# Attention with projections for two problems: weight reloads split by head group, V loads moved to SP's queue, a new order of the first loads

## The chip, the core and the metric

The kernel runs on one core of a Trainium2 chip. Its time is the device time of one execution in microseconds; the median of several executions is compared. TensorE, VectorE, ScalarE and GpSimd (PE, DVE, ACT and POOL in the profile) compute; SyncE (SP) only issues transfers. SP, ACT and POOL each issue DMAs in the order of their own instruction stream, and a wait in such a stream holds everything behind it.

## The reference

Two independent problems A and B of the same shape. Each has 8 batches of 160 queries of width 448, a projection to 16 heads of width 256, cached K and V of 512 positions for each batch and head, and a projection back to 448. All tensors are bfloat16. The results stand side by side in the output (8, 160, 896).

```
q = (x @ wq) -> (B, H, Sq, Dh)
scores = einsum("bhqd,bhkd->bhqk", q, k_cache) * Dh ** -0.5
o = einsum("bhqk,bhkd->bhqd", softmax(scores), v_cache)
out = o -> (B, Sq, H*Dh) @ wo
```

## The kernel before

**Units.** The work is cut into 64 units. A unit is one batch and one head group (4 heads). Two batches form a group (8 units: 4 head groups x 2 batches); problem A has groups 0 to 3, problem B groups 4 to 7. A unit needs one K block (1 MB, loaded by two transposing DMAs, one for each half of the head width, L263) and one V block (1 MB, one copy, L283). K has 6 buffers (`NK`) and is issued 5 units ahead (`DK`); V has 3 buffers (`NV`) and is issued 2 units ahead (`DV`).

**Steps.** The program is written out by hand as one list of tasks for each engine, a loop over steps U = 0 to 63. In step U TensorE computes the scores of unit U (L426, two halves of each head), and between them the product of probabilities and V of unit U-1 (L475 for 128 queries, L500 for the other 32), its row sums (L479, L506), the transposes of the normalised result of unit U-2 (L524, L548), up to 8 chunks of the query projection for the coming group (L320, one chunk is 128 columns of wq), and at the end of the step the output projection of a unit pair three steps back (L358). ScalarE takes the exponential (L439), VectorE empties the accumulators.

**Weights.** One buffer holds wq (`wq_sb`) and one wo (`wo_sb`), for the problem that is being computed. wq of A is loaded by ACT as the first thing (L160, L162). wo of A is issued by SP at step 0, behind the first six K blocks. Problem B's weights replace them: all of wq in 16 DMAs at step 25 (`RELOAD_STEP + 1`, issued by SP when all 128 chunks of problem A are projected), with the chunks of group 4 held back to step 29; all of wo in two halves when every output projection of A is done. One semaphore counts all of wq of a problem and one all of wo, so a consumer waits for the whole matrix.

**Queues.** SP issues K, wq of B and wo. POOL issues x, V and the output. V of unit U waits, on POOL, for its buffer (`pv_done`) and for K of the same unit (`k_sems`):

```
            if U in k_req:
                ksl_, kval_ = k_req[U]
                waits.append((k_sems[ksl_], kval_))
```

**The start.** ACT issues wq, POOL issues x of group 0 and then sets up the identity and ones tiles. SP first waits until wq has landed and then issues K of units 0 to 5 and wo; V of units 0 and 1 follows on POOL. TensorE transposes x of group 0 (L228 and L230, large and small pieces in turn), VectorE copies it (L240, L241), and 8 chunks of the query projection come before the first scores.

Of the kernel before, what the change touches and what calls it, by code (L numbers as in the profile page):

```python
# [33 lines left out]
def bass_concat_heads__mha_block_cached__gqa_block_cached__near_ridge_kernel(  # L34
# [20 lines left out]
    with ExitStack() as es:  # L55
# [42 lines left out]
        oacc_done = S("oacc_done")  # L98
        k_sems = [S(f"k_sem{i}") for i in range(NK)]
        x_sems = [S("x_sem0")]  # L100
        xtr_done = S("xtr_done")
        xevac_done = S("xevac_done")
        wq_sems = [S("wq_sem0"), S("wq_sem1")]
        v_sems = [S(f"v_sem{i}") for i in range(NV)]
        wo_sem = S("wo_sem")
        out_sems = [S("out_sem0")]
        id_sem = S("id_sem")

# [37 lines left out]
                               base=0, pattern=[[-1, 128]], channel_multiplier=1).then_inc(id_sem, 1)  # L146
            pool.memset(wq_sb[0:64, 3, :], 0.0).then_inc(id_sem, 1)

        wq_need = {0: 16 * 4 * 1, 1: 16 * 4 * 4}

        def load_wq(prob_i, cs=(0, 1, 2, 3), split=1):
            prob = probs[prob_i]
            WQB = HD // split

            def body(eng):
                for c in cs:
                    for kb in range(split):
                        cols = slice(kb * WQB, (kb + 1) * WQB)
                        if c < 3:
                            eng.dma_start(wq_sb[:, c, cols], prob["wq"][c * 128:(c + 1) * 128, cols]).then_inc(wq_sems[prob_i], 16)  # L160
                        else:
                            eng.dma_start(wq_sb[64:128, c, cols], prob["wq"][D - 64:D, cols]).then_inc(wq_sems[prob_i], 16)  # L162
            return body

        def load_wo(prob_i, qs=(0, 1, 2, 3)):
            prob = probs[prob_i]

            def body(pool):
                for q in qs:
                    pool.dma_start(  # L170
                        wo_sb[:, q * 8:(q + 1) * 8, :],
                        prob["wo"][q * 1024:(q + 1) * 1024, :].rearrange("(hd p) n -> p hd n", p=128),
                    ).then_inc(wo_sem, 16)
            return body

        x_uses = [0]
# [2 lines left out]
        def issue_x_dma(g):  # L179
            if g >= NGROUPS or ("dma", g) in xg_emitted:  # L180
                return
            xg_emitted[("dma", g)] = True
            prob = probs[g // NG_PER_PROB]
            gb = g % NG_PER_PROB
            xb2 = 0
            waits = []
            if g - 1 >= 0:
                waits.append((xtr_done, g - 1 + 1))
            x_uses[xb2] += 1
            need = 16 * 2 * BG * x_uses[xb2]  # L190

            def body(pool):
                for bl in range(BG):
                    b = gb * BG + bl
                    pool.dma_start(xn_sb[:, xb2, bl, 0, :], prob["x"][b, 0:128, :]).then_inc(x_sems[xb2], 16)
                    pool.dma_start(xn_sb[0:SQ - 128, xb2, bl, 1, :], prob["x"][b, 128:SQ, :]).then_inc(x_sems[xb2], 16)
            task("pool", waits, body)
            return need

        x_need = {}  # L200
# [1 line left out]
        def issue_x(g):  # L202
            if g >= NGROUPS or ("tr", g) in xg_emitted:
                return
            xg_emitted[("tr", g)] = True
            xb2 = 0
            xb = g % NX
            slots = []
            waits = [(x_sems[xb2], x_need[g]), (id_sem, 2)]
            for k2 in range(2):  # L210
                w_, slot = pj_waits()
                waits += w_
                pj_hist.append(("x", g))
                cnt["pj"] += 1
                slots.append(slot)
            if g - NX >= 0:
                waits.append((qproj_done, 32 * (g - NX + 1)))
            pA = pj_banks[slots[0]].bitcast(dt.bfloat16)
            pB = pj_banks[slots[1]].bitcast(dt.bfloat16)

            def pe_body(pe):
                last = None
                for c in range(4):
                    c0 = c * 128 if c < 3 else D - 128
                    dst = pA if c < 3 else pB
                    cb = (c if c < 3 else 0) * NCOL
                    for bl in range(BG):
                        last = pe.transpose(dst[:, cb + bl * SQ:cb + bl * SQ + 128],  # L228
                                            xn_sb[:, xb2, bl, 0, c0:c0 + 128], ident[:, :])
                        last = pe.transpose(dst[:, cb + bl * SQ + 128:cb + (bl + 1) * SQ],  # L230
                                            xn_sb[0:SQ - 128, xb2, bl, 1, c0:c0 + 128], ident[0:SQ - 128, 0:SQ - 128])
                last.then_inc(xtr_done, 1)
            task("pe", waits, pe_body)

            dwaits = [(xtr_done, g + 1)]
            if g - NX >= 0:
                dwaits.append((qproj_done, 32 * (g - NX + 1)))

            def dve_body(dve):
                dve.tensor_copy(xT_sb[:, xb, 0:3, :], pA[:, 0:3 * NCOL].rearrange("p (c n) -> p c n", c=3))  # L240
                dve.tensor_copy(xT_sb[:, xb, 3, :], pB[:, 0:NCOL]).then_inc(xevac_done, 1)  # L241
            task("dve", dwaits, dve_body)
# [21 lines left out]
            task("sp", waits, body)  # L264

        def issue_v(U):
            if U >= NUNITS:
                return
            g, u, hg, bl, prob, b = unit_info(U)
            sl = U % NV  # L270
            waits = []
            if U - NV >= 0:
                waits.append((pv_done, 5 * (U - NV + 1)))
            if U in k_req:
                ksl_, kval_ = k_req[U]
                waits.append((k_sems[ksl_], kval_))
            v_uses[sl] += 1
            v_req[U] = (sl, 16 * v_uses[sl])

            def body(pool):  # L280
                dst = v_sb[:, sl, :, :]
                src = prob["v"][b, hg * HG:(hg + 1) * HG, :, :].rearrange("h (p j) d -> p h (j d)", j=4)
                pool.dma_start(dst, src).then_inc(v_sems[sl], 16)  # L283
            task("pool", waits, body)

        wo_gen = {}

        def pj_waits():
            i = cnt["pj"]
# [13 lines left out]
        def q_chunk(gq, hd):  # L303
            xb = gq % NX
            waits, slot = pj_waits()
            waits.append((xevac_done, gq + 1))
            waits.append((wq_sems[gq // NG_PER_PROB], wq_need[gq // NG_PER_PROB]))
            waits.append((id_sem, 3))
            qi = cnt["qchunk"]
            assert qi // 32 == gq, (qi, gq)  # L310
# [25 lines left out]
        def out_proj(g, hg):  # L336
# [4 lines left out]
            for t in tiles:  # L341
                waits, slot = pj_waits()
                waits.append((otevac_done, 2 * last_unit + 2))
                waits.append((wo_sem, wo_gen[g]))
                oi = cnt["otile"]
                otile_idx[(g, hg, t)] = oi
                pj_hist.append(("o", oi))
# [214 lines left out]
                dve.tensor_copy(o_t, i_t).then_inc(otevac_done, 1)  # L562
            task("dve", dwaits, dve_body)

        for g in range(NGROUPS):
            wo_gen[g] = 64 * (1 + g // NG_PER_PROB)

        task("act", [], load_wq(0))
        x_need[0] = issue_x_dma(0)
        task("pool", [], pool_init)  # L570
        x_need[1] = issue_x_dma(1)
        task("sp", [(wq_sems[0], wq_need[0])], lambda sp: None)
        for U in range(max(DK, DV)):
            if U < DK:
                issue_k(U)
            if U < DV:
                issue_v(U)
        task("act", [(id_sem, 1)], lambda act: act.activation(warm_sb[:, :], ones_sb[:, :], ACTF.Exp, scale=SCALE))
        issue_x(0)
        for hd in range(8):  # L580
# [5 lines left out]
        for gq in range(1, NGROUPS):  # L586
            for hd in range(NHD):
                hgq = hd // 8
                min_step = unit_index(gq - 1, hgq, BG - 1) + 1
                q_queue.append([gq, hd, min_step])  # L590
        RELOAD_STEP = unit_index(NG_PER_PROB - 1, 0, 0)
        for e_ in q_queue:
            if e_[0] == NG_PER_PROB:
                e_[2] = max(e_[2], RELOAD_STEP + 5)
        wq_reloaded = False
        wo_reloaded = False
        oproj_pending = [(g, hg) for g in range(NGROUPS) for hg in range(NHG)]
# [1 line left out]
        for U in range(NUNITS):  # L599
            g, u, hg, bl, prob, b = unit_info(U)  # L600
            cnt["step"] = U
            issue_k(U + DK)
            if U == RELOAD_STEP + 1:
                assert all(not (e_[0] < NG_PER_PROB) for e_ in q_queue), "problem-0 chunks still pending"
                task("sp", [(qevac_done, 32 * NG_PER_PROB)], load_wq(1, (0, 1, 2, 3), split=4))
                wq_reloaded = True
            if U == 0:
                task("sp", [], load_wo(0))
            issue_v(U + DV)
            if u == 2 and g + 2 < NGROUPS:  # L610
                x_need[g + 2] = issue_x_dma(g + 2)
            step_chunks = []
# [23 lines left out]
            for i_ in range(per_block[HG]):  # L636
                q_chunk(*step_chunks.pop(0))
            assert not step_chunks
            while oproj_pending:
                pg, phg = oproj_pending[0]  # L640
                extra = 3 if (pg == NG_PER_PROB and phg == 0) else 0
                if unit_index(pg, phg, BG - 1) + 3 + extra <= U:
                    out_proj(pg, phg)
                    oproj_pending.pop(0)
                else:
                    break
            if wo_reloaded is False and all(((NG_PER_PROB - 1, hh_, 2) in otile_idx) for hh_ in range(NHG)):
                task("sp", [(oacc_done, cnt["oacc"])], load_wo(1, (0, 1)))
                wo_reloaded = U
            elif (wo_reloaded is not False and wo_reloaded is not True):  # L650
                task("sp", [], load_wo(1, (2, 3)))
                wo_reloaded = True

        assert not q_queue
        U = NUNITS
# [6 lines left out]
        otr_tail_task(U - 1)  # L662
        for (pg, phg) in list(oproj_pending):
            out_proj(pg, phg)
        assert wo_reloaded and wq_reloaded

        def final_wait(sp):
            sp.wait_ge(out_sems[0], 16 * out_dma_count[0])
# [43 lines left out]
```

## Time and profile before

| | us |
|---|---|
| median of 6 runs | 707.13 |
| lowest and highest run | 701.29, 726.39 |
| the profiled execution | 695.91 |
| its span | 694.1 |
| TensorE busy in the span | 656.3 (95%) |
| VectorE busy | 443.3 (64%) |
| ScalarE busy | 220.2 (32%) |
| bytes moved by DMA, mean rate | 154.77 MB, 223 GB/s |

The profiled execution is one execution; its own time is 1.8 us longer than the span, which runs from its first to its last recorded instruction. A busy TensorE is not one at its peak: matmuls are pipelined, and its clock can be halved for some microseconds (the PEclk column, 1.00 is the full clock). q1 is the DMA queue of SP, q10 that of ACT, q0 that of POOL. A row "SPq L263" is the time that SP spends on issuing one transposing DMA[...].

### The profile page before, as it was taken

What the parts mean: (1) busy time and instruction counts of PE and PEld (TensorE: products, weight loads), DVE (VectorE), ACT (ScalarE), POOL (GpSimd) and SP (SyncE); (2) the same over time, 40 slices, a digit from 0 to 9 for tenths busy, and PEclk for the clock granted to TensorE, in tenths of its full rate; (3) what the DMA queues carried; (4) which work ended last, traced back from release to release, by engine and by line L of the source; (5) the groups of instructions that cost most, each with busy time, mean ns of one, the idle gap of its engine ahead of it and who ended that gap; (6) DMA issues with size and microseconds to landing.
All of it is one profiled execution on the core that took longest, in us unless ns stands there. A gap on an engine that the chain in (4) does not pass through costs nothing.

```text
span 694.1 us, 19606 instructions
## 1 busy us (share of the span) xinstructions
PE 656.3 (95%) x8576; PEld 521.2 (75%) x8576; DVE 443.3 (64%) x1120; ACT 220.2 (32%) x514; POOL 86.4 (12%) x136
## 2 busy tenths in 40 slices
PE   3799599999999999998999999999999999999985
PEld 1578478787787788786877788778777887788862
DVE  1457457676676667665666677667676667676662
ACT  0223233332333333252322344233323333334420
POOL 4002000020000300020000220002000020001001
PEclk9979989999999999999999999999999999999999
DMA  8999999999999999999999999999999999999500
GB/s 259 224 190 238 299 236 219 242 262 220 246 221 268 242 230 235 213 321 180 185 245 236 233 264 292 247 227 215 262 242 244 199 240 150 222 245 225 173 7 21
DMA packets 297174, 154.77 MB, mean 223 GB/s; under 512 B 268736, under 2 KB 277440, under 8 KB 296640
## 3 DMA queue, kind: packets, MB, share of 16 engines
q1 hardware_dynamic: 276608, 78.14, 70.7%
q0 software_dynamic: 19968, 71.70, 32.8%
q10 hardware_dynamic: 512, 3.67, 1.5%
q8 instruction: 68, 1.11, 0.7%
q14 instruction: 18, 0.15, 0.1%
HBM read 84.08 MB, written 2.29 MB: 124 GB/s over the span
## 4 chain that ended last, share of the span: by engine, by line
PE 85%; SPq 8%; DMA 4%; DVE 1%; issue 1%; POOL 0%; ACTq 0%; POOLq 0%
PE ps L426 20%; PE ps L358 18%; PE ps L320 17%; PE ps L475 15%; SPq L263 8%; PE ps L500 5%; PE ps L524 4%; PE ps L479 3%; DMA wo_sb<-in_A_wo_dram 2%; DMA wq_sb<-in_A_wq_dram 2%; PE ps L548 1%; PE ps L228 1%; PE ps L230 1%; SPq L170 1%; PE ps L506 1%
## 5 line engine op out<-in xcount | busy, mean ns | idle before, releaser
L439 ACT ACTIVATE pT_sb<-ps 128x320 bf16<-128x320 f32 x512 | 218.7, 437 | 447.2 <-PE ps L426 446.4
L426 PE MATMUL ps<-qT_sb,kT_sb 128*128 128x160 bf16 x2048 | 221.4, 235 | 5.1 <-DMA kT_sb<-in_A_k_cache_dram 2.8
L320 PE MATMUL ps<-xT_sb,wq_sb 128*128 128x320 bf16 x1024 | 170.0, 306 | 3.7 <-DVE xT_sb L241 2.7
L426 PEld LDWEIGHTS ps<-qT_sb,kT_sb 128*128 128x128 bf16 x2048 | 154.5, 114 | 14.1 <-DMA kT_sb<-in_A_k_cache_dram 3.5
L457 DVE TENSOR_SCALAR ob_sb<-ps,rc_sb 128x256 bf16<-128x256 f32 x320 | 154.9, 484 | 11.2
L475 PE MATMUL ps<-v_sb,pT_sb 128*128 128x256 bf16 x1024 | 154.6, 274 | 1.3 <-DMA v_sb<-in_A_v_cache_dram 1.3
L330 DVE CAST qT_sb<-ps 128x320 bf16<-128x320 f32 x256 | 125.6, 490 | 38.7 <-PE ps L320 33.9
L320 PEld LDWEIGHTS ps<-xT_sb,wq_sb 128*128 128x128 bf16 x1024 | 95.7, 100 | 35.0 <-DVE xT_sb L241 2.9
L358 PE MATMUL ps<-wo_sb,oT_sb 128*128 128x448 bf16 x512 | 103.9, 357 | 7.9 <-DMA wo_sb<-in_A_wo_dram 7.9
L455 DVE RECIPROCAL rc_sb<-ps 128x1 f32<-128x1 f32 x320 | 53.9, 168 | 80.7 <-PE ps L479 58.3
L475 PEld LDWEIGHTS ps<-v_sb,pT_sb 128*128 128x128 bf16 x1024 | 93.1, 98 | 7.5 <-DMA v_sb<-in_A_v_cache_dram 1.4
L358 PEld LDWEIGHTS ps<-wo_sb,oT_sb 128*128 128x128 bf16 x512 | 50.0, 99 | 52.8 <-issue 10.7
L479 PEld LDWEIGHTS ps<-ones_sb,pT_sb 128*128 128x128 bf16 x1024 | 63.5, 97 | 6.1
L479 PE MATMUL ps<-ones_sb,pT_sb 128*128 128x4 bf16 x1024 | 62.3, 165 | 0.0
L283 POOL DMA_DIRECT2D v_sb<-in_A_v_cache_dram x32 | 24.2, 756 | 282.3 <-PE ps L506 149.7
L283 POOL DMA_DIRECT2D v_sb<-in_B_v_cache_dram x32 | 24.2, 755 | 266.1 <-PE ps L506 226.8
L374 DVE TENSOR_TENSOR oacc_sb<-ps,oacc_sb 128x448 f32<-128x448 f32 x40 | 25.0, 625 | 37.4 <-PE ps L358 37.4
L534 DVE COPY oT_sb<-ps 128x1024 bf16<-128x1024 bf16 x64 | 44.2, 691 | 2.6 <-PE ps L524 0.8
L500 PE MATMUL ps<-v_sb,pT_sb 128*32 128x256 bf16 x1024 | 39.7, 275 | 0.0
L524 PE MATMUL ps<-ident,ob_sb 128*128 128x128 bf16 x512 | 39.1, 219 | 0.5 <-DVE oTt_sb L562 0.5
L524 PEld LDWEIGHTS ps<-ident,ob_sb 128*128 128x128 bf16 x512 | 32.6, 98 | 3.0 <-issue 0.6
L372 DVE COPY oacc_sb<-ps 128x448 f32<-128x448 f32 x20 | 12.5, 625 | 28.3 <-PE ps L358 28.3
(31 smaller groups left out, 241.1 us busy)
## 6 DMA issues: line engine op xcount, KB each, us to landing
v_sb<-in_A_v_cache_dram POOLq DMA_DIRECT2D x32, 1024.0 KB, 8.1
v_sb<-in_B_v_cache_dram POOLq DMA_DIRECT2D x32, 1024.0 KB, 8.1
wo_sb<-in_A_wo_dram SPq DMA_DIRECT2D x4, 896.0 KB, 11.9
wo_sb<-in_B_wo_dram SPq DMA_DIRECT2D x4, 896.0 KB, 8.9
wq_sb<-in_A_wq_dram ACTq DMA_DIRECT2D x3, 1024.0 KB, 7.7
wq_sb<-in_B_wq_dram SPq DMA_DIRECT2D x12, 256.0 KB, 4.9
out_dram<-out_sb POOLq DMA_DIRECT2D x16, 112.0 KB
kT_sb<-in_A_k_cache_dram SPq DMA_TRANSPOSE x64, 8.8
```

What stands on the lines that cost most here:

```text
L263: sp.dma_start_transpose(kT_sb[:, sl, dh, :], src).then_inc(k_sems[sl], 16)
L320: last = pe.matmul(pjb[:, 0:NCOL], wq_sb[:, c, hd * 128:(hd + 1) * 128], xT_sb[:, xb, c, :], start=(c == 0), stop=(c == 3))
L330: dve.tensor_copy(qT_sb[:, hd, :], pjb[:, 0:NCOL]).then_inc(qevac_done, 1)
L358: last = pe.matmul(pjb[0:M, 0:D], stat, wo_sb[:, hd, :], start=(i8 == 0), stop=(i8 == 7))
L426: last = pe.matmul(scb[:, jj * SQ:(jj + 1) * SQ], kt, qT_sb[:, 2 * head + dh, bl * SQ:(bl + 1) * SQ], start=(dh == 0), stop=(dh == 1))
L439: act.activation(pT_sb[:, psl, 2 * half:2 * half + 2, :], scb[:, 0:2 * SQ].rearrange("p (a s) -> p a s", a=2), ACTF.Exp, scale=SCALE).then ...
L455: dve.reciprocal(rc_sb[:, rci:rci + 1], obk[:, DH:DH + 1]).then_inc(rc_sem, 1)
L457: dve.tensor_scalar(out=ob_sb[:, obuf, tile, :], in0=obk[:, 0:DH], scalar1=rc_sb[:, rci:rci + 1], scalar2=None, op0=ALU.mult).then_inc(nor ...
L475: pe.matmul(obk[:, 0:DH], pT_sb[:, psl, jv, 0:128], v_sb[:, vsl, h, jv * DH:(jv + 1) * DH], start=(jv == 0), stop=(jv == 3))
L479: last = pe.matmul(obk[:, DH:DH + NSUM], pT_sb[:, psl, jv, 0:128], ones_sb[:, 0:NSUM], start=(jv == 0), stop=(jv == 3))
L500: pe.matmul(obk[32 * h:32 * (h + 1), 0:DH], pT_sb[:, psl, jv, 128:SQ], v_sb[:, vsl, h, jv * DH:(jv + 1) * DH], start=(jv == 0), stop=(jv = ...
L524: last = pe.transpose(otr_bank[:, (2 * k + dh) * 128:(2 * k + dh + 1) * 128], ob_sb[:, obuf, k, dh * 128:(dh + 1) * 128], ident[:, :])
```

## The change

1. **V moves from POOL to SP** (`issue_v`), and its wait for K of the same unit is dropped. V of unit U now stands in SP's stream directly behind K of unit U+3.
2. **The start is reordered.** x of group 0 is issued by SP as its first DMAs, with a semaphore of its own; K of unit 0 follows without a wait for wq; then SP waits for wq, and V0, K1, V1, V2, K2, wo, K3 and K4 follow. Step 0 adds K5 and step 1 adds K6 and V3.
3. **The reload of wq** is split by head group (`wqB_sem0` to `3`): the four DMAs of head group kb are issued one step after the last chunks of group 3 that read those columns. The projections of group 4 are no longer held back to step 29.
4. **The reload of wo** is split by head group in the same way (`woB_sem0` to `3`), each one step after group 3's output projection of that head group. The output projection of group 4's first head group is no longer held back by three steps.
5. **The transposes of x** are sorted: first the eight large pieces, then the eight small ones.

```diff
-        wq_need = {0: 16 * 4 * 1, 1: 16 * 4 * 4}
-        def load_wq(prob_i, cs=(0, 1, 2, 3), split=1):
+        def load_wq(prob_i, sem, kbs=(0, 1, 2, 3), coarse=False):
...
+                for kb in (kbs if not coarse else (None,)):
+                    cols = slice(kb * WQB, (kb + 1) * WQB) if kb is not None else slice(0, HD)
+                    for c in range(4):
...
-                    pool.dma_start(
+                    sem = wo_sems[0] if prob_i == 0 else woB_sems[q]
+                    eng.dma_start(
...
+            if g == 0:
+                sem, eng_key = x0_sem, "sp"
+                need = (x0_sem, 16 * 2 * BG)
...
-            if U in k_req:
-                ksl_, kval_ = k_req[U]
-                waits.append((k_sems[ksl_], kval_))
...
-                pool.dma_start(dst, src).then_inc(v_sems[sl], 16)
-            task("pool", waits, body)
+                sp.dma_start(dst, src).then_inc(v_sems[sl], 16)
+            task("sp", waits, body)
...
-            waits.append((wq_sems[gq // NG_PER_PROB], wq_need[gq // NG_PER_PROB]))
+            if gq // NG_PER_PROB == 0:
+                waits.append((wq_sems[0], 16 * 4))
+            else:
+                waits.append((wqB_sems[hd // 8], 16 * 4))
...
-                waits.append((wo_sem, wo_gen[g]))
+                waits.append((wo_sems[0], 16 * 4) if g // NG_PER_PROB == 0 else (woB_sems[hg], 16))
...
-        task("act", [], load_wq(0))
         x_need[0] = issue_x_dma(0)
+        task("act", [], load_wq(0, wq_sems[0], coarse=True))
         task("pool", [], pool_init)
         x_need[1] = issue_x_dma(1)
-        task("sp", [(wq_sems[0], wq_need[0])], lambda sp: None)
-        for U in range(max(DK, DV)):
-            if U < DK:
-                issue_k(U)
-            if U < DV:
-                issue_v(U)
+        issue_k(0)
+        task("sp", [(wq_sems[0], 16 * 4)], lambda sp: None)
+        issue_v(0)
+        issue_k(1)
+        issue_v(1)
+        issue_v(2)
+        issue_k(2)
+        task("sp", [], load_wo(0))
+        for U in range(3, DK):
+            issue_k(U)
...
-            if U == RELOAD_STEP + 1:
-                task("sp", [(qevac_done, 32 * NG_PER_PROB)], load_wq(1, (0, 1, 2, 3), split=4))
-            if U == 0:
-                task("sp", [], load_wo(0))
             issue_v(U + DV)
+            for kb in wq_phase_pending.pop(U, []):
+                last_chunk = max(qchunk_idx[(LASTG0, hd_)] for hd_ in range(kb * 8, kb * 8 + 8))
+                task("sp", [(qevac_done, last_chunk + 1)], load_wq(1, wqB_sems[kb], (kb,)))
+            for kb in wo_phase_pending.pop(U, []):
+                task("sp", [(oacc_done, cnt["oacc"])], load_wo(1, (kb,)))
...
-                extra = 3 if (pg == NG_PER_PROB and phg == 0) else 0
+                extra = 0
```

## The prediction

> **What bounds the kernel now.** I read the page's busy row first, then TensorE's waits, then the table by stage, then the chain that ended last for the first 90 us.
>
> ```profile
> PE 656.3 (95%) x8576; PEld 521.2 (75%) x8576; DVE 443.3 (64%) x1120; ACT 220.2 (32%) x514; POOL 86.4 (12%) x136
> ```
>
> TensorE is busy for 656.3 of 694.1 us. So only its 37.8 us of gaps, and stretches at a reduced clock, can be won. The waits of TensorE name the gaps (us in total, times, longest):
>
> ```profile
> PE ps L228 <- DMA xn_sb<-in_A_x_dram: 9.7, 1, 9.7
> PE ps L358 <- DMA wo_sb<-in_A_wo_dram: 7.9, 1, 7.9
> PE ps L426 <- DMA kT_sb<-in_A_k_cache_dram: 2.8, 2, 2.5
> PE ps L426 <- issue: 2.3, 1, 2.3
> PE ps L475 <- DMA v_sb<-in_A_v_cache_dram: 1.3, 1, 1.3
> ```
>
> All but the fourth lie before 87 us. By stage (columns: stage and length, busy us of PE, PEld, DVE, ACT, POOL, then PEclk, DMA share, GB/s):
>
> ```profile
> 14.20:31.00 16.80, 13.91 (x96) 9.16 (x96) 7.87 (x16) 3.06 (x8) 1.61 (x3) 1.00 1.07 215
> 31.00:43.30 12.30, 10.02 (x61) 6.65 (x62) 3.18 (x8) 1.75 (x4) 1.51 (x2) 0.58 1.15 230
> 43.30:78.80 35.50, 35.50 (x498) 29.75 (x496) 27.77 (x70) 12.25 (x28) 4.41 (x7) 1.00 1.16 229
> 78.80:87.00 8.20, 0.34 (x3) 0.01 (x1) 0.88 (x2) 0.00 (x0) 0.00 (x0) 0.83 1.12 310
> 87.00:92.00 5.00, 4.95 (x16) 2.11 (x17) 0.62 (x1) 0.00 (x0) 0.00 (x0) 0.60 1.17 221
> 196.90:277.50 80.60, 80.58 (x1089) 64.68 (x1080) 55.38 (x141) 27.45 (x65) 11.26 (x18) 1.00 1.10 241
> ```
>
> Read it in two halves. In a steady group (last row, eight units of one batch and four heads) TensorE is busy for 80.58 of 80.60 us at full clock: 10.1 us a unit, and no transfer shows in it. Up to 87 us transfers set the pace, and SP's queue is the chain that ended last (start, us):
>
> ```profile
> 15.59 3.24 SPq L263
> 18.89 2.66 SPq L263
> 21.59 2.12 SPq L263
> ...
> 36.98 2.43 SPq L263
> 39.46 2.25 SPq L263
> 41.75 10.67 SPq L263
> ...
> 73.24 13.68 DMA wo_sb<-in_A_wo_dram
> ```
>
> One L263 row is one half of a K unit (0.52 MB, transposed by the DMA). With no V in flight a half takes 2.1 to 2.7 us, so I price K at 2 x 2.4 = 4.8 us. At 41.75 one half takes 10.67 us; the DMA view of 44:48 and that of 72:76 tell why:
>
> ```profile
> DMA packets 190, 0.28 MB, mean 70 GB/s; under 512 B 130, under 2 KB 130, under 8 KB 190
> ```
> ```profile
> DMA packets 2082, 1.46 MB, mean 364 GB/s; under 512 B 620, under 2 KB 2082, under 8 KB 2082
> ```
>
> The first has a K transpose on SP's queue (q1) and a V copy on POOL's (q0) in flight together and moves 70 GB/s. The second has K and then wo on q1 alone, and moves 364.
>
> **The change, part by part.** *V goes from POOL to SP, without its wait for K.* POOL's waits for K (100.0 and 39.3 us in its waits) disappear. K, V, wo and the reloads stand in one line, so K and V can't meet on two queues. V (1.05 MB) at 364 GB/s is 2.9 us. From copy back to transpose I add 1.3 us, read at 85.5 to 87, where wo ends and the next K begins (24 GB/s for about 1 us). A steady unit then asks 4.8 + 2.9 + 1.3 = 9.0 us of the ring against TensorE's 10.1: hidden, with 1.1 us of cover. SP's own waits for TensorE (201.4 us in 49) hold the 64 more issues at 0.4 to 0.6 us each, as wo's first ones have. The new wait for pv_done in SP's stream has the next K behind it; that K is due five units (50 us) later, so nobody waits.
>
> *x(0) goes to SP, first of all.* It may land near 5 us (wq's first piece, issued at 0.74, has landed at about that time). Transposes (2.9 us) and the copy to xT_sb (1.0) follow, but the first projection waits for wq, which lands at 14.2. Gain 0, with 5 us of cover. Its four issues (0.4 to 0.6 us each) hold K(0) back to about 2.9 us; POOL's set-up starts 2.3 us earlier, and later x loads and outputs no longer stand behind V on POOL: 0, nobody waits for them after 10 us. Sorting the 16 transposes into big and small ones: 0.
>
> *K(0) no longer waits for wq.* Bounds: it gets nothing while wq flows (0), or it runs in wq's slack, at most its 4.8 us. The last pieces of wq come slower than the first, so I take 1.5 us of gain for the ring. TensorE gains nothing: K(0) is wanted at 21.8 when eight projections are done. A page of the Trainium skill speaks to this place, "DMA: Bandwidth & Descriptors", in "Queues, rings and completion order": a DMA engine takes its queues in turn, packet by packet. By that rule two queues lose no bandwidth by meeting, and the early K(0) costs at most its own share. The row of 44:48 says otherwise: 70 GB/s while both were in flight. By the rule the ring is on time; by the row it loses what the next rival costs. I take the rule here, as most meetings in this trace were no such crawl, and keep the row as that rival.
>
> *The prologue's order.* SP now has x0, K0, (wq), V0, K1, V1, V2, K2, wo, K3, K4, K5, K6, V3. From 14.2 us, at 4.8 for K, 2.9 for V and 3.67 MB / 364 GB/s = 10.1 for wo: K0 19.0, V0 21.9, K1 26.7, V2 32.5, K2 37.3, wo 47.4, K3 52.2, K6 66.6, V3 69.5. With x(1) on POOL (0.8), three steps from copy to K (3.9) and the head start (-1.5), V3 lands at 73. TensorE: first scores 21.8, step 0 ends at 28.2 and finds K1; V0 is there; step 1, 17.9 us now, loses its 1.4 us wait and the 5.1 us that 10.2 us at half clock cost (31:43.3), and ends at 39.6; step 2 ends at 49.6 (10.0). K3 comes at 54 or a little later, step 3 ends near 64. Then **V3 is late by 9 us: the wait for wo becomes a wait for V3**, which is wanted at the start of step 4 and not at its end. From there step 4 has 9.9 us of work before its output projection, 3.0 for that, and about 2 for half clock after the stall (5.14 against 3.03 now): step 5 starts at 73 + 14.9 = 87.9, now 92.0. V4 follows one unit (9.0) behind V3, at 82, so nothing is late next. **Gain 4.1 us**, out of the 19 that the stalls and their clock cost now.
>
> The clock rule I checked: "TensorE: Matmul & The Clock Gate" (The HAM clock gate) has the half rate follow an idle window of about 3.4 us. Here waits of 2.5 and 1.3 us near 30 us were followed by 10.2 us at half rate. By the rule K3's wait of 4 us costs its half rate and one of 2 us none; by the row either may cost 2 to 5 us, but before V3 all of it is hidden by V3.
>
> *wq and wo are reloaded by head group.* The same bytes, in four pieces of 0.92 MB between units, not in one block of 3.67 MB at 295 us. At that block's end two K halves took 25.8 us:
>
> ```profile
> 305.00 25.78 SPq L263 DMA_TRANSPOSE kT_sb<-in_A_k_cache_dram  x2
> ```
>
> There TensorE had its 2.3 us of "issue" (at 327.1) and then 3.4 us at half clock, 1.7 us lost. I count both as won: **4.2 us** with the 0.2 about it. Lower bound 0 (an issue gap need not be the block's), upper 4.2. The projections of group 4 move up from step 29 to 26; no work is added. Each piece costs SP's ring 2.5 + 1.3 us, within the 1.1 us of cover of three or four units, and V has two steps (20 us) to land.
>
> **Sum.** 4.1 + 4.2 = 8.3 us. The profiled execution's 695.91 us becomes 687.6. The median, 707.13, is 11.2 us above that execution; I carry the same difference over: **698.8 us**, 1.2% below. About 1% is what a measurement of this kernel can tell from no change.
>
> **Rivals.**
> - *The ring runs at the old rate.* 14.2 to 87 us moved about 235 GB/s. The 15.5 MB up to V3 then land at 14.2 + 66 = 80, step 5 at 95: 3 us lost, 4.2 won, about 706. For it: two thirds of these bytes are still transposes. Against: no second queue interferes.
> - *Slower: K(0) crawls beside wq.* Two queues meet from 3 to 14 us, copy and transpose. If that repeats what 305 us shows (25.8 us for 4.8 us of K, of which other traffic explains 8 to 13), the ring is 8 to 21 us late; at 18 V3 lands at 91 and step 5 starts at 106: +14 - 4.2, about 717. It loses to no change from V3 at 81 on. Against: the crawl is seen in few places, though wq has no pause.
> - *More gain.* The shown runs reach 726 where the profile has 696; if collisions of two queues make that spread, one ring takes it away, and the prologue may be bound by TensorE alone: 19 + 4.2 us, about 684.
> - *The steady state becomes bound by the ring*, at over 10.1 us a unit: it needs 1.1 us more a unit than I count, and then costs up to 38 us if each change of kind took 1.5 us both ways. In 72:76 the first change is seen without a gap, so I leave this within the slower case.
>
> **Chances.** Forecast 0.45 (its own range 692 to 706, three quarters of it beyond 1%), old rate 0.18, more gain 0.17, slower 0.20. Faster 0.34 + 0.17 = 0.51, same 0.11 + 0.18 = 0.29, slower 0.20. The range runs from just below "more gain" to the crawl: 681 to 717.
>
> **What would show it.** Right: no wait for wo; one TensorE wait for v_sb near 63 to 73 us; step 5 near 88; the stall at 327 gone; V's landing near 5 us in the steady state with no TensorE wait. Wrong: wq landing well after 14.2 (crawl); TensorE waits for kT_sb or v_sb after 100 us (ring bound); a busy PE sum that grows.

## The result, and the profile after

The changed kernel takes 688.32 us (median of 5 runs, 683.36 to 688.92), the kernel before 704.49 us (10 runs). The ratio is **0.9793, 95% interval 0.9731 to 0.9854**. In a later set of runs (experiment 12) it was 0.9870 (0.9816 to 0.9925). Some executions are more than 1.5% longer than the shortest of their kernel, up to 726.39 us here, and the ratios leave these out, so that they are not the quotients of the medians. The profiled executions differ by less than the medians: 695.91 before, 688.42 after (span 686.6), 7.5 us; the one before is among the shortest of its kernel, the one after is a middling one.

The page's first row and TensorE's waits of the kernel after (us in total, times, longest):

```profile
PE 644.4 (94%) x8576; PEld 516.6 (75%) x8576; DVE 443.3 (65%) x1120; ACT 220.0 (32%) x514; POOL 35.9 (5%) x68
```
```profile
PE ps L237 <- DMA xn_sb<-in_A_x_dram: 10.6, 1, 10.6
PE ps L485 <- DMA v_sb<-in_A_v_cache_dram: 6.6, 1, 6.6
PE ps L436 <- DMA kT_sb<-in_A_k_cache_dram: 5.6, 1, 5.6
PE ps L485 <- DMA v_sb<-in_B_v_cache_dram: 3.8, 1, 3.8
PE ps L330 <- issue: 2.5, 1, 2.5
```

TensorE is busy for 11.9 us less, though it executes the same 8576 matmuls. The wait for wo is gone; a wait for V of problem A and one for K stand in its place. The second wait for V (3.8 us) is new and lies at 431 us. The last row is the wait at 14 us, where wq lands. The table by stage of the kernel after (columns as before):

```profile
49.70:55.60 5.90, 0.34 (x4) 0.03 (x2) 0.86 (x2) 0.00 (x0) 0.00 (x0) 0.91 1.26 185
68.60:75.40 6.80, 0.19 (x3) 0.01 (x1) 0.46 (x2) 0.44 (x1) 0.00 (x0) 0.72 1.09 239
193.20:272.40 79.20, 79.18 (x1092) 63.91 (x1076) 55.36 (x140) 27.39 (x64) 5.18 (x10) 1.00 1.13 232
431.20:435.20 4.00, 0.27 (x4) 0.08 (x2) 0.63 (x2) 0.44 (x1) 0.00 (x0) 0.77 1.13 285
435.20:441.00 5.80, 5.72 (x44) 4.47 (x44) 2.37 (x6) 0.87 (x2) 0.00 (x0) 0.57 1.06 224
```

The first two rows are K of unit 3 and V of unit 3 at the start. The third is the surprise: a steady group takes 79.20 us, where it took 80.60, and TensorE is busy throughout in both cases. The last two are the new wait and the low clock behind it.

Against the prediction, step by step (us; a step starts with its first row of scores in the timeline):

| | before | predicted | after |
|---|---|---|---|
| step 0 starts | 21.8 | 21.8 | 21.9 |
| step 1 starts | 31.0 | 28.2 | 28.4 |
| step 2 starts | 48.9 | 39.6 | 39.8 |
| step 3 starts (K of unit 3) | 58.9 | 54 or a little later | 55.6 |
| V of unit 3, first use | 69.2 | 73 | 75.4 |
| step 5 starts | 92.0 | 87.9 | 89.6 |
| a steady group (units 16 to 23) | 80.6 | as before | 79.2 |
| group 3, with the reload of wq | 84.6 | 80.4 | 79.2 |
| group 5 (units 40 to 47) | 80.5 | as before | 86.1 |

The 7.5 us of the profile are made up as follows. The start gains 2.4. Groups 1 to 6 gain 1.4 each, 8.4 in all; in them the x transposes of groups 2 to 7 are done. Group 3 gains 4.0 more, as its stall is gone. The wait at 431 us with its clock costs 6.9. What is left, some -0.4, are small stalls and the end.

### The profile page after: what moved, and what is told of

The parts are those of the page before. It is cut to its first block, busy times and chain, and to the rows that moved or that the text cites. A ratio compares the mean times of both kernels' runs of the same rounds, so it can differ in the third digit from the quotient of the medians.

```text
span 686.6 us, 19551 instructions
## 1 busy us (share of the span) xinstructions
PE 644.4 (94%) x8576; PEld 516.6 (75%) x8576; DVE 443.3 (65%) x1120; ACT 220.0 (32%) x514; POOL 35.9 (5%) x68
## 4 chain that ended last, share of the span: by engine, by line
PE 86%; SPq 8%; DMA 4%; DVE 1%; issue 0%; POOL 0%; POOLq 0%
PE ps L436 21%; PE ps L330 18%; PE ps L368 17%; PE ps L485 15%; SPq L274 7%; PE ps L510 5%; PE ps L534 4%; PE ps L489 3%; DMA v_sb<-in_B_v_cache_dram 2%; PE ps L558 1%; DMA v_sb<-in_A_v_cache_dram 1%; DMA kT_sb<-in_A_k_cache_dram 1%; SPq L172 1%; PE ps L516 1%; DVE ob_sb L467 0%; PE ps L237 0%
## 5 line engine op out<-in xcount | busy, mean ns | idle before, releaser
L485 PE MATMUL ps<-v_sb,pT_sb 128*128 128x256 bf16 x1024 | 154.9, 274 | 10.5 <-DMA v_sb<-in_A_v_cache_dram 6.6
L485 PEld LDWEIGHTS ps<-v_sb,pT_sb 128*128 128x128 bf16 x1024 | 93.1, 98 | 17.3 <-DMA v_sb<-in_A_v_cache_dram 6.8
L368 PE MATMUL ps<-wo_sb,oT_sb 128*128 128x448 bf16 x512 | 102.1, 352 | 0.0
L510 PEld LDWEIGHTS ps<-v_sb,pT_sb 128*32 128x32 bf16 x1024 | 21.4, 96 | 12.0 <-DVE ob_sb L467 7.9
L368 PE MATMUL ps<-wo_sb,oTt_sb 128*128 128x448 bf16 x128 | 26.8, 352 | 0.0
```

Of the source, the lines that this page charges most:

```text
L368: last = pe.matmul(pjb[0:M, 0:D], stat, wo_sb[:, hd, :], start=(i8 == 0), stop=(i8 == 7))
L485: pe.matmul(obk[:, 0:DH], pT_sb[:, psl, jv, 0:128], v_sb[:, vsl, h, jv * DH:(jv + 1) * DH], start=(jv == 0), stop=(jv == 3))
L510: pe.matmul(obk[32 * h:32 * (h + 1), 0:DH], pT_sb[:, psl, jv, 128:SQ], v_sb[:, vsl, h, jv * DH:(jv + 1) * DH], start=(jv == 0), stop=(jv = ...
```

## Experiments

Twelve runs were made, in three sets (1 to 4, 5 to 8, 9 to 12), each on a chip of its own with its own runs of the kernel before. The changed kernel itself ran again only in the third set, and its two ratios, 0.9793 and 0.9870, show how far sets can differ. The second set has no ratio.

**1. Sorting the x transposes, alone.** The changed kernel's loop over `tail` put into the kernel before.

```diff
+                for tail in (0, 1):
...
-                        last = pe.transpose(dst[:, cb + bl * SQ:cb + bl * SQ + 128],
...
+                            if tail == 0:
+                                last = pe.transpose(dst[:, cb + bl * SQ:cb + bl * SQ + 128],
```

> The kernel before, with one part of the change alone: the eight large transposes of x first, then the eight small ones. The prediction priced this at 0. New theory, from the two traces: sixteen transposes in turn start over 2.27 us (130.69 to 132.80 and the last one), sorted over about 0.9 us, so 1.35 us a group; six of the eight groups (2 to 7) have nothing behind which to hide it, which is 8.1 us: ratio 0.9885, median near 696. Rival (the prediction's price): no change, ratio 1.000, the 1.4 us per steady group that the trace after shows coming from the queues instead.

Measured: ratio 0.9921 (0.9869 to 0.9973), median 697.88 us (688.39 to 738.56). In the profile the three of groups 1 to 6 that hold no stall (2, 4 and 5) take 79.1 to 79.2 us; the other three take 83.9, 88.2 and 89.1. Group 2 by table:

```profile
194.30:273.50 79.20, 79.18 (x1092) 63.91 (x1074) 55.36 (x140) 27.40 (x64) 11.26 (x18) 1.00 1.16 237
```

The timeline shows why. Before, a pair of transposes starts every 0.28 us (the first two of eight pairs, and the work that follows):

```profile
130.69 0.22 PE L228 MATMUL ps<-ident,xn_sb 128*128 128x128 bf16 x1
130.84 0.18 PE L230 MATMUL ps<-ident,xn_sb 32*128 32x32 bf16 x1
130.96 0.23 PE L228 MATMUL ps<-ident,xn_sb 128*128 128x128 bf16 x1
131.12 0.18 PE L230 MATMUL ps<-ident,xn_sb 32*128 32x32 bf16 x1
...
132.92 0.62 PE L524 MATMUL ps<-ident,ob_sb 128*128 128x128 bf16 x8
```

Eight such pairs take 2.23 us. In the changed kernel all sixteen fit in 0.84 us:

```profile
128.26 0.61 PE L237 MATMUL ps<-ident,xn_sb 128*128 128x128 bf16 x8
128.81 0.36 PE L240 MATMUL ps<-ident,xn_sb 32*128 32x32 bf16 x8
129.10 0.62 PE L534 MATMUL ps<-ident,ob_sb 128*128 128x128 bf16 x8
```

So a change between a 128-row and a 32-row operand costs 0.10 us on average: 1.4 us for the 14 of 15 changes that sorting removes. The expected ratio, 0.9885, is within the interval, and the prediction's 0 is outside.

**2. The same part undone.** The changed kernel with the old loop.

> The changed kernel with the transposes of x in the old order, large and small in turn. If sorting is worth 1.35 us a group: 8.1 us more than the changed kernel, about 696 us, and steady groups of 80.6 us again. If the gain of the steady groups comes from V having left POOL: within 1 us of the changed kernel, about 688 us.

Measured: 692.63 us (690.58 to 693.45), ratio 0.9933 (0.9907 to 0.9959). Groups 1 to 6 take 80.6 us each again; group 2, in a window that ends 0.1 us early:

```profile
196.50:277.00 80.50, 80.48 (x1080) 64.60 (x1072) 55.37 (x140) 27.39 (x64) 5.19 (x10) 1.00 1.08 223
```

V's queue does not matter for that number. The median is 4.3 us above that of the changed kernel and not 8.1; in the profile the wait at 431 us is absent. TensorE's unit of 10.1 us leaves the ring (SP's queue) more time than one of 9.9, but only just: V of unit 39 lands 0.1 us ahead of its use.

**3. V ahead of K.**

```diff
-            issue_k(U + DK)
             issue_v(U + DV)
+            issue_k(U + DK)
```

> The changed kernel with the two calls at the head of a step exchanged: V of unit U+2 is issued ahead of K of unit U+5. Theory: TensorE's new wait for V at 431 us (3.8 us, and half clock behind it until 440.2) is a V that stands behind a K with some 25 us to spare on a ring that the reloads fill; with V first it has 4.8 us more and the wait goes (5 to 6 us), and V of unit 3 lands 4.8 us earlier than 75.4, so step 5 starts near 85: about 678 us. Rival: the ring as a whole is too slow in the reload stage, whatever its order; then a wait for K or V of about 4 us stays near 431 us and only the start gains: about 683 us.

The profiled execution, 677.01 us, is the shortest of six and did as the theory says: no wait at 431 us, step 5 at 84.8, groups 1 to 6 at 79.2 each. But the median is 689.19 us (677.01 to 697.93), no shorter than the changed kernel's, and the ratio, 0.9766, rests on two executions (0.9629 to 0.9903). So a gain over the changed kernel isn't shown by the times. In the profile V of unit 39 had only 0.2 us to spare. Why the runs differ from each other stays open.

**4. V back on POOL's queue, all else as in the change.**

```diff
-            task("sp", waits, body)
+            task("pool", waits, body)
```

> The changed kernel with V back on POOL's queue, with its old wait for K of the same unit; all else as in the change. Theory of one queue: K and V meet on two queues again, some stretches crawl, and the runs spread and rise as those of the kernel before do: about 697 us, the spread over 10 us. Rival: the queue of V does not matter and the rest of the change carries the gain: 681 to 688 us, the wait for V at 431 us gone and the spread below 6 us.

Measured: 687.10 us (681.98 to 698.74), ratio 0.9845 (0.9764 to 0.9925). The spread is over 10 us, as the theory of one queue says. In time that can't be told from the changed kernel, so that theory falls as to the size. But the losses are others: step 5 starts at 80.3, as V of unit 3 no longer stands behind K and wo, and the waits for V are gone. Instead TensorE stands still for 8.8 us at 370 us and 4.9 us at 267 us with no releaser ("issue"). The table row and the DMA lines of the longer one:

```profile
369.67:378.70 9.03, 0.23 (x3) 0.11 (x2) 0.65 (x2) 0.00 (x0) 0.00 (x0) 0.71 1.26 59
```
```profile
DMA packets 1376, 0.53 MB, mean 59 GB/s; under 512 B 1332, under 2 KB 1332, under 8 KB 1375
...
q1 hardware_dynamic: 1328, 0.34, 116.1%
q0 software_dynamic: 47, 0.18, 7.7%
q8 instruction: 1, 0.02, 2.5%
```

K (q1) and V (q0) crawl at 59 GB/s together, and one instruction fetch (q8) falls in that stretch.

**5. V first and K only 3 units ahead (DK = 3).**

> V first as in the run before, and K only 3 units ahead of its use instead of 5 (DK = 3). Theory: V had 0.2 to 1.5 us to spare near 410 to 460 us while K had over 20; two K fewer ahead of each V give V 9.6 us more, and K keeps some 10 us. Then no TensorE wait for V or K after 100 us and runs within 4 us of each other; the start gains by V of unit 3 landing ahead of K of unit 5 and 6, the wait for K of unit 3 behind wo (6 us) stays: 671 to 675 us in all runs. Rival: K is now the one that comes late, with waits for kT_sb in the reload stage, 685 us or more.

Measured: 683.97 us (679.08 to 688.46). Half of the rival came true: no wait for V is left, but TensorE now waits for K in several places (after the start 2.1 us at most, near 404 us; group 4 takes 83.7 us). The reserve had been moved from V to K, and was too small in sum.

**6. The same, with wo behind the first K blocks.**

```diff
-        task("sp", [], load_wo(0))
         for U in range(3, DK):
...
+            if U == 1:
+                task("sp", [], load_wo(0))
```

> As the run with V first and DK = 3, and the four loads of problem A's wo moved behind K of unit 4, into step 1. Theory: wo is wanted at the end of step 4 and K of unit 3 at the start of step 3; with wo 10 us later on the ring K of unit 3 lands near 44 us and wo near 65, so that TensorE waits for nothing after the first projection and step 5 starts at 73 to 76: about 664 us, 8 to 10 us below the other run. Rival: the ring as a whole is the bound of the start, so the 6 us wait for K turns into one of the same size for wo or V before 90 us: 670 to 675 us.

Measured: 684.15 us (678.70 to 686.43), no shorter than experiment 5 and far from the expected 664. Steps 3, 4 and 5 start at 50.4, 60.4 and 73.5, as worked out; then K of unit 6, behind wo, makes TensorE wait for 3.8 us near 79 us, and waits for K in the reload stage take back the rest.

**7. Block reloads on one ring.** The changed kernel with wq of B in one block, wo in two halves.

> The changed kernel with the reloads as they were: all of problem B's wq in one block at step 25 and group 4's projections held back to step 29, wo in two halves after the last output projection of problem A, group 4's first output projection three steps later. The prediction's step counted 4.2 us for the split. Theory now: on one ring the stall at 327 us of the kernel before (an instruction gap in a crawl of two queues) does not come back, but a block of 10 us and more stands ahead of V, whose spare time near 290 us is 6 to 9 us; TensorE waits for V or for wq by 3 to 10 us: 689 to 698 us. Rival: the split is worth nothing, the same waits in sum: 684 to 689 us.

Measured: 692.66 us (692.34 to 694.93). TensorE's waits for V:

```profile
PE ps L485 <- DMA v_sb<-in_A_v_cache_dram: 10.1, 2, 7.0
...
PE ps L485 <- DMA v_sb<-in_B_v_cache_dram: 2.8, 1, 2.8
```

One is the start's (7.0), one is 3.1 us at 319 us, one 2.8 us at 424 us. No "issue" gap at 327 us comes back, although the block does. The median is about 5 us above the changed kernel's, but stage by stage the profile does not lay these on the reloads: groups 3 to 5 take 244.9 us here and 244.7 in the first profile of the changed kernel (238.4 in that of experiment 12). The start (step 5 at 91.7) and the end, which the split doesn't touch, are each 2 to 3 us longer.

**8. No reloads.** Problem B is computed with problem A's weights; 7.3 MB of loads are left out.

```diff
-                task("sp", [(qevac_done, last_chunk + 1)], load_wq(1, wqB_sems[kb], (kb,)))
...
-                task("sp", [(oacc_done, cnt["oacc"])], load_wo(1, (kb,)))
```

> The changed kernel without the reload of wq and wo: problem B is computed with problem A's weights, so 7.3 MB of loads are left out. Theory: the reload pieces (3 to 4 us each of ring time, eight of them in 16 steps) are what uses up V's spare time; without them V keeps 8 us or more to spare at every unit, the wait for V at 431 us goes with its half clock, and the groups all take 79.2 us: 679 to 681 us. Rival: the ring without reloads is slower than TensorE too, or a crawl makes the wait: some wait for V stays, 685 us or more.

Measured: 683.73 us (681.17 to 686.68), 3 us above what was expected; profiled 682.58. Groups 1 to 6 take 79.2 us each, and TensorE's only waits for V and K are those of the start:

```profile
PE ps L485 <- DMA v_sb<-in_A_v_cache_dram: 6.5, 1, 6.5
PE ps L436 <- DMA kT_sb<-in_A_k_cache_dram: 5.5, 1, 5.5
```

Each V of units 24 to 48 lands 11.9 us or more ahead of its first use. In the changed kernel that reserve is 9.3 us at unit 24 and 0.0 at unit 37. So the reload pieces are what uses it up.

**9. K 4 units ahead, V first, wo later.**

> V first, wo behind the last K of the prologue, and K 4 units ahead (DK = 4), the middle between the runs with 5 and with 3. Theory: with 5 ahead V ran out of spare time near unit 39 (0.2 us) while K had 20; with 3 ahead K ran out (waits of 9.5 us in 6 places) while V had 3 and more; at 4 ahead both keep 4 us or so, the ring's total of about 11 us a unit in the reload stage is carried by the buffers, and no TensorE wait over 2 us is left after the start: 670 us, runs within 6 us. Rival: the ring's shortage in the reload stage is larger than both reserves together and a wait of 3 to 8 us stays: 676 to 682 us.

Measured: 679.36 us (672.89 to 687.96), ratio 0.9728 (0.9661 to 0.9795). This is the rival's case: TensorE still waits for V, 2.4 us at 298 us and 4.5 us at 403 us.

**10. K for two units at a time.**

```diff
+            issue_v(U + DV)
+            if U == 1:
+                task("sp", [], load_wo(0))
+                issue_k(5)
+            elif U == 3:
+                for k_ in (6, 7, 8):
+                    issue_k(k_)
+            elif U % 2 == 1:
+                issue_k(U + 4)
+                issue_k(U + 5)
```

> V first and wo behind the prologue's K, and K issued for two units at a time in every second step, so that the ring carries V V K K V V K K where it lags. Theory: a unit takes 9.1 us of the ring in the changed kernel, of which 4.8 us are K by its clean halves and 2.9 us V, so about 1.3 us are the turn from copy to transpose; with half as many turns a unit takes 8.4 us, the reload stage 10.3 us instead of 11, and nothing waits: 668 us. Rival: the turn does not cost that, or K in pairs comes late at its second half: 675 us and more.

Measured: **670.61 us (667.77 to 672.62), ratio 0.9640 (0.9610 to 0.9670)**, the fastest of all. TensorE's waits, and the table from the second half of the first problem through all reloads:

```profile
PE ps L436 <- DMA kT_sb<-in_A_k_cache_dram: 4.2, 2, 2.8
```
```profile
182.90:262.10 79.20, 79.18 (x1085) 63.87 (x1074) 55.34 (x140) 27.39 (x64) 5.19 (x10) 1.00 1.00 222
262.10:420.40 158.30, 158.26 (x2152) 127.66 (x2144) 110.69 (x280) 54.78 (x128) 8.46 (x16) 1.00 1.14 261
```

In the second row (units 24 to 39) the same ring moves 261 GB/s and TensorE never waits. V keeps 3.5 us or more to spare there, K 15. While the ring catches up after the start, from K of unit 9 to K of unit 17, two units land 17.3 us apart on average (106.7 to 175.7); in the changed kernel 18.3 us (99.1 to 172.2). That is about 1 us saved for the one turn in two units that goes, near the 1.3 us expected. Experiment 9, with V first and wo later but a turn for each unit, is the nearest to compare: 679.36 us. K's lead differs between the two as well, so the whole of the 8.75 us isn't shown to be the turns.

**11. Sorted transposes and one queue, old start and block reloads.**

> The kernel before with the sorted transposes and with V on SP's queue without its wait for K; order of the start and block reloads as before. It stands against the run with sorted transposes alone. Theory: the waits that the trace calls issue (11.2, 2.2 and 1.9 us there) belong to stretches in which a K on one queue and a V on another crawl and an instruction fetch is late; on one queue they go, and the runs draw together (under 8 us from lowest to highest against 50). V of unit 2 stands behind six K and wo in the start, so the start is late by about 5 us; near 320 us V waits behind the block: 690 to 697 us. Rival: the issue waits stay although one queue carries all: then they have another cause, and the spread stays above 15 us.

Measured: 697.98 us (696.98 to 699.88), ratio 1.0037 (1.0015 to 1.0059). Against experiment 1, which has the same sorting and start order but two queues (0.9921, 0.9869 to 0.9973), that is about 1.2% slower. It is less sure than the intervals say, as sets differ by 0.8% and the medians (697.98 and 697.88) don't differ. The executions do draw together as expected: 2.9 us from the lowest to the highest, against 50 in experiment 1. The two kernels lose their time in different places, TensorE's waits of experiment 1 first, then of this one:

```profile
PE ps L324 <- issue: 11.2, 3, 6.5
PE ps L362 <- DMA wo_sb<-in_A_wo_dram: 10.7, 1, 10.7
...
PE ps L430 <- issue: 2.2, 2, 1.7
PE ps L479 <- issue: 1.9, 1, 1.9
```
```profile
PE ps L476 <- DMA v_sb<-in_A_v_cache_dram: 21.7, 2, 14.6
...
PE ps L321 <- issue: 3.5, 1, 3.5
```

The last row is the wait for wq at the start; in the first fence 3.1 of the 11.2 us are the same. The "issue" gaps of the middle go, and waits for V take their place: 14.6 us at the start, where V stands behind six K and wo, and 7.1 us later in problem A (21.7 less 14.6).

**12. The changed kernel again.**

> The changed kernel once more, beside the three others on their chip: 683 to 689 us by its first runs; steady groups of 79.2 us, and a wait for V of 3 to 7 us in one place between 380 and 480 us.

Measured: 687.50 us (681.91 to 694.53), ratio 0.9870. The steady groups take 79.2 us; the wait for V is shorter than expected:

```profile
PE ps L485 <- DMA v_sb<-in_B_v_cache_dram: 0.7, 1, 0.7
```

It is the same wait near 431 us, 3.8 us in the first profile: it lies on an edge. Group 5 takes 80.1 us here and 86.1 there.

## Why the prediction was right, and where it was not

The forecast was 8.3 us less than the profiled execution, and the profiled executions differ by 7.5 us. That they lie so near is luck: two terms put at nothing nearly cancel (8.4 us won, 6.9 lost), and a third came true for another reason than the one given. For the median, forecast at 698.8 us, the direction held and the size did not: it is 688.32, below the forecast's own range of 692 to 706 and within the whole range of 681 to 717.

- **From the profile to the median: 11.2 us carried over.** After the change this difference is gone (688.32 against 688.42), and so the median was missed by 10.5 us. The rival "more gain" named it: one ring takes the spread away. The runs point that way (2.9 us from lowest to highest in experiment 11, 50 in experiment 1), but on one ring too the spread is 12.6 us in experiment 12 and 20.9 in experiment 3. What makes the long executions isn't shown.
- **V to SP.** Right that K and V on one ring don't crawl. Stretches of 4 us in which the DMA engines are busy and move under 75 GB/s lie at three to five places in each of the three profiles with two queues (before, 1 and 4), and at one place at most in each of the eleven others. TensorE's issue gaps of over 2 us in the middle of the kernel are in the same three alone. But no gain of the whole kernel follows from the queue: experiment 4, with two queues, can't be told from the changed kernel in time (0.9845 against 0.9793 and 0.9870), and experiment 11, with one queue and the old start order, is not faster than experiment 1. One ring in order brings waits for V in exchange.
- **The ring's price of a unit**, 9.0 us, was measured as about 9.1 (18.3 for two). **The failed step is the one after it**: each reload piece "within the 1.1 us of cover of three or four units". There are eight pieces in about sixteen steps, one in two steps and not one in four. By the prediction's own numbers they ask 8 x 3.8 = 30 us where sixteen units give 18, and sorting shrank the cover to 0.8 x 16 = 13. Between K of unit 25 and K of unit 41 two units took the ring 21.5 us on average (18 to 23), and TensorE 19.8. V's reserve paid the rest and ran out at units 37 to 39, which cost 6.9 us with the clock in the first profile and 0.9 in the second. Experiment 8 shows it by taking the pieces away, and in the profile of experiment 3 the order alone avoids the wait. A TensorE wait for v_sb after 100 us was the prediction's own sign of being wrong here, and it came.
- **Sorting the transposes: 0** was wrong. It is 1.4 us for each group that TensorE bounds, 8.4 us in all (experiments 1 and 2), the largest term of the change. The prediction had looked only at the first group, where wq hides it. With it falls the premise that only gaps and reduced clock can be won: the busy time itself fell, by 11.9 us.
- **The start.** The order was followed to within 2.4 us, and the wait for wo did become waits for K and then V of unit 3. The gain was 2.4 us instead of 4.1. Step 5 starts at 89.6 in the changed kernel, at 80.5 with V first and K 3 ahead (experiment 5), and at 73.5 with wo later as well (experiment 6): 16 us from the order of issues, 7 of them from wo. Up to this step not the bytes bounded the start, but their order. In experiment 9 most of it lasts: unit 8 starts at 99.5 us, in the changed kernel at 114.1.
- **The split reloads: 4.2 us.** The stall at 327 us is gone, but not for the reason given, and this term came true by luck. With the block on one ring the stall stays away too (experiment 7), and with the split on two queues such gaps come elsewhere (experiment 4). What the split itself is worth on one ring isn't shown: between 0.2 and 6.5 us by groups 3 to 5.
- **K(0) beside wq.** The page's rule was the right choice: wq landed by 14.4 us and K(0) at 19.5, no crawl. The same rule would have corrected the x(0) step, which was put near 5 us and which came at 10.6. The DMA view of 4:9 after the change:

```profile
q10 hardware_dynamic: 263, 1.89, 90.9%
q1 hardware_dynamic: 245, 0.18, 10.7%
```

  There are almost as many packets from each queue, as taking turns would give; but those of ACT's data (wq) have 8 KB and those of SP's (x) 896 bytes, so x gets a tenth of the rate. It cost nothing, behind wq.
- **The clock.** The wait of 3.8 us at 431 us brought half clock from 433.4 to 440.2, as the page's rule (an idle window of about 3.4 us) would have it. But the length of one wait alone doesn't decide: in experiments 6, 7 and 10 waits of 1.8, 2.8 and 2.8 us also came with 3.4 us of half clock, and one of 3.1 us in experiment 7 with none.

## What to carry to other kernels

When several streams go to one in-order DMA queue, add up what each stage asks of it, one-time loads included, and compare the sum with the stage's compute. The block that has the smallest reserve should stand first, not the one that is issued furthest ahead. Try putting like next to like on that queue: V first, wo later and fewer turns between transposes and copies took 2.5% off the changed kernel here (670.61 against 687.50 us), about half of it with the pairs (679.36 without), and no byte was saved for it. And price an edit in the stage where its engine is the bound, not in the one where the trace first shows it.

## What the runs showed of the hardware that was not expected

- Sixteen TensorE transposes of 128 and of 32 rows in turn take 2.23 us, the same sixteen sorted by size 0.84 us.
- Two DMA queues with work moved 263 and 245 packets in the same 5 us; with packets of 8 KB on one and of 896 bytes on the other, the second got a tenth of the bandwidth (0.18 against 1.89 MB).
- On one queue, two units of K and V took about 1 us less where the ring turns back from copies to transposes once (experiment 10) and not twice (17.3 against 18.3 us).
- A transposing K stream and a copy stream on two queues can fall to 59 to 70 GB/s, and TensorE stood without a releaser for up to 8.8 us there, with an instruction fetch in that stretch. There are 68 fetches in experiment 4's 689.5 us, one in 10 us; the one in this gap came 20.5 us after the fetch before it, and that in the longest gap of experiment 1 (6.5 us) 20.9. That the late fetch is what stops TensorE is inferred from this; it was not tried by itself. What starts such a crawl is open: K(0) beside wq, and most meetings of K and V, showed none.
